# Row table of a fused attention and routed MLP kernel: wide one-hots on two engines, later and more spread out; casts and loads moved

## The chip, the cores and the metric

One core of a Trainium2 chip runs the whole program. The metric is the device time of one execution in microseconds (us), lower is better. The engines are PE (TensorE, matmul), DVE (VectorE), ACT (ScalarE), POOL (GpSimd) and SP (SyncE, which only issues DMAs here). Each engine runs its own instructions strictly in program order and waits on semaphores for the others.

## The reference

```python
B, H, S, D = 8, 8, 576, 64              # batch, heads, sequence, head size
scores = q @ k.T / sqrt(D)              # per batch and head
mask = (row // 64) >= (col // 64)       # block causal, blocks of 64
attn = softmax(where(mask, scores, -1e9))
x = (attn @ v) -> rows of tokens, N = 4608 rows of 512
expert = token_ids * 2654435761 % 8     # 8 experts
out[rows of e] = relu(x[rows of e] @ w1[e]) @ w2[e]   # 512 -> 1024 -> 512
```

Inputs are float32 (token ids int64), the output is float32 [4608, 512].

## The kernel before

The program has two stages. Attention writes its result as bf16 rows to `x_dram`; the expert stage then gathers the rows of each expert in groups of 128 by an index table, `perm3` (128 x 72 integers: one column for each group of 128 slots), multiplies by the two weight matrices and scatters the rows to the output.

**Attention** runs over 32 pairs of heads, `g = 4 b + pr` (batch `b`, pair `pr` of that batch); the loop has 34 steps, because the second half of a pair's work is done two steps later. All engines follow the order in which the code is written (a manual schedule), so a step is a row of instructions in each engine's queue:

- PE: `S_chunk(g, 0..2)` (scores, in PSUM tile `ps`), between them `PV(g-2, 0..1)` (probabilities times V, into the single PSUM tile `O`), at `pr == 0` `S_rest(b)` (the last 64 rows of all four pairs), then `T_pair(g+2)` (transposes q and k of the pair after next into PSUM tile `tp`).
- ACT: one exponential for each chunk (L286), and the two of `S_rest` (L301), once in each batch.
- DVE: `norm(g-2)` (L343 a reciprocal, L346 two multiplications, into tile `xs`), the copy of `tp` into `qkT` (L231), parts of the token routing, casts of q and k of the next batch from float32 to bf16 (L169, L174, tiles `qb` and `kb`), half of the cast of V (L181).
- POOL: the other half of the cast of V (L182, L183, into `vx`; L189 once in each batch), and the DMAs that write a finished batch of `xs` to `x_dram` (`write_x`, L356 and L358, four steps' work in one go at `pr == 1` of the next batch).
- SP: the loads of q, k and v. One batch is 3.54 MB of float32. Each of the tiles `qf`, `kf`, `vf` has two buffers, so that a load of batch b + 2 waits until the casts of batch b have read theirs. A load of `kf` is two DMAs of 512 KB (L109) and two of 64 KB (L116, the last 64 rows).

**Routing** turns the token ids into slots. `route()` is a generator, cut by `yield` into pieces: experts of all tokens, a running count (L399), base offsets through two small matmuls (L407, L408), and the slot number of each token, split into column `shi` (slot // 128) and row `slo` (slot % 128). Then `place(b)`, one call for each batch b, builds `perm3`: for each of five groups of up to 128 tokens it makes a one-hot of the row (`ohp`, 128 x 128, L497) and two of the column times the token number's high and low part (`ohg`, 128 x 72, L499 twice), and a matmul of the two adds each token number to its place; L505 adds the sum of the batch to `acc`. That is 16 DVE instructions and 5 matmuls in one step. `placed()` turns `acc` into `perm3`.

In the order of the steps, `route()` has its first piece ahead of the loop and the others in steps 0 to 3, `place(0)` to `place(7)` are in steps 4 to 11, and `placed()` is in step 12. The loads of q and k of batch 1 are issued ahead of the loop, and the first casts of batch 1 (L169, L174) are in step 0. Ten buffers `xg` for the gathered rows are set to zero on POOL at the very start (L535).

```python
        if g + 2 < NPAIRS:
            T_pair(g + 2)
        if g < 4:
            next(rgen, None)
        elif g < 4 + B:
            place(g - 4)
        elif g == 4 + B:
            placed()
```

Of the kernel before, what the change touches and what calls it, by code (L numbers as in the profile page):

```python
# [7 lines left out]
ALU = mybir.AluOpType  # L8
# [26 lines left out]
def kernel(  # L35
# [334 lines left out]
    def route():  # L370
# [7 lines left out]
        pr = psO.tile([P, 2, 512], F32, name="O", tag="O")[:, 0, 0:325].rearrange("p (i d) -> p i d", i=5)  # L378
        for i in range(5):
            n = P if i < NT else 64  # L380
            nc.tensor.matmul(pr[0:n, i, 0:B], lhsT=eb[:, 128 * i : 128 * i + n],
                             rhs=identbf[0:B, 0:B], start=True, stop=True)
# [4 lines left out]
        nc.vector.tensor_copy(et[0:64, NT, :], pr[0:64, NT, 0:B])
        T = 5 * B
        etf = et[:].rearrange("p i b -> p (i b)")
# [55 lines left out]
        nc.vector.tensor_copy(shi[:], sj[:])  # L445
        nc.vector.tensor_single_scalar(sj[:], si[:], 127, op=ALU.bitwise_and)
        nc.vector.tensor_copy(slo[:], sj[:])

        tokf = rt.tile([P, 5, B], F32, name="tokf")
        nc.gpsimd.iota(tokf[:], pattern=[[P, 5], [S, B]], base=1, channel_multiplier=0,  # L450
                       allow_small_or_imprecise_dtypes=True)
        pidx = rt.tile([P, 1], F32, name="pidx")
        cidx = rt.tile([P, 1], F32, name="cidx")
        nc.gpsimd.iota(pidx[:], pattern=[[0, 1]], base=0, channel_multiplier=1,
                       allow_small_or_imprecise_dtypes=True)
        for c in range(4):
            nc.gpsimd.memset(cidx[32 * c : 32 * c + 32, :], float(c))

        inner = rt.tile([P, 1], F32, name="inner")
        nc.vector.tensor_single_scalar(cidx[:], cidx[:], -127.0, op=ALU.mult)  # L460
        nc.vector.scalar_tensor_tensor(out=inner[:], in0=pidx[:], scalar=4.0, in1=cidx[:],
                                       op0=ALU.mult, op1=ALU.add)
        tok = rt.tile([P, 5, B], I32, name="tok")
        tj = rt.tile([P, 5, B], I32, name="tj")
        nc.vector.tensor_scalar(tok[:, 0:NT, :], tokf[:, 0:NT, :], inner[:, 0:1], None, op0=ALU.add)
        nc.vector.tensor_scalar(tok[:, NT, :], tokf[:, NT, :], pidx[:, 0:1], None, op0=ALU.add)
# [14 lines left out]
        nc.vector.tensor_single_scalar(tj[:], tok[:], 6, op=ALU.arith_shift_right)  # L481
        nc.vector.tensor_copy(vhi[:], tj[:])
        nc.vector.tensor_single_scalar(tj[:], tok[:], 63, op=ALU.bitwise_and)
        nc.vector.tensor_copy(vlo[:], tj[:])
# [52 lines left out]
    load_qk(0, 0, 2, rest=False, engs=(nc.sync, nc.scalar))  # L537
    load_qk(0, main=False, engs=(nc.sync, nc.scalar))
    load_qk(0, 2, 8, rest=False, engs=(nc.sync, nc.scalar))
    load_v(0)  # L540
# [225 lines left out]
```

## Time and profile before

| | |
|---|---|
| median of 3 runs | 375.94 us (374.07 to 376.49) |
| the profiled execution | 375.76 us |
| its span, first to last instruction | 374.1 us |
| busy: PE / DVE / ACT / POOL | 290.7 / 187.8 / 147.0 / 165.7 us |
| exponentials, first start | 19.02 us |
| exponentials, last end | 185.86 us |
| first gather of the expert stage, start | 201.97 us |
| bytes moved by DMA | 64.60 MB |

The profiled execution took 375.76 us, 1.66 us more than its span; the rest lies around the first and last instruction. The expert stage starts when the last rows of attention are in `x_dram`, so the table splits the span into attention (up to about 200 us) and the expert stage (about 174 us). In attention, the exponentials of L301 mark the batches: they stand at the end of step 4b.

### The profile page before, as it was taken

How to read it: one execution, taken by the hardware profiler on the slowest of the kernel's cores; microseconds unless marked ns; L12 is line 12 of the kernel's file. 1: busy time of each engine (PE TensorE's matmuls, PEld its weight loads, DVE VectorE, ACT ScalarE, POOL GpSimd, SP SyncE). 2: the span in 40 equal slices, each digit the busy share in tenths (PEclk: the TensorE clock that was granted, in tenths of full speed). 3: DMA queues.
4: the chain of work that ended last, by engine and by line, in shares of the span. 5: the costliest groups of instructions: out<-in, count | busy, mean ns of one | idle time of the engine just before them, and what ended most of it. 6: DMA issues, size and time to landing. Idle time of an engine off the chain costs nothing. (4 is left out here: it accounts for less than half of the span.)

```text
span 374.1 us, 8170 instructions
## 1 busy us (share of the span) xinstructions
PE 290.7 (78%) x3311; PEld 210.1 (56%) x3311; DVE 187.8 (50%) x496; ACT 147.0 (39%) x177; POOL 165.7 (44%) x249
## 2 busy tenths in 40 slices
PE   0356677777668996989920799999999999999992
PEld 0234454455446774766720489495958586767640
DVE  7767977666776995869430220404141313232141
ACT  1054433344434996788910055050414132322300
POOL 6136106200800754739424724737465655614252
PEclk9999556567666999899995599999999999999997
DMA  8999695059226898968722399869696969744532
GB/s 193 300 260 257 151 288 133 11 154 225 66 91 163 196 256 194 277 166 169 157 52 75 90 179 224 206 178 203 190 206 187 194 213 196 222 98 141 129 135 83
DMA packets 67047, 64.60 MB, mean 173 GB/s; under 512 B 19378, under 2 KB 60340, under 8 KB 64960
## 3 DMA queue, kind: packets, MB, share of 16 engines
q0 software_dynamic: 12288, 35.71, 40.0%
q1 hardware_dynamic: 52064, 27.17, 29.1%
q10 hardware_dynamic: 2656, 1.18, 1.3%
q8 instruction: 26, 0.43, 0.5%
q14 instruction: 13, 0.11, 0.1%
HBM read 67.15 MB, written 15.20 MB: 220 GB/s over the span
## 5 line engine op out<-in xcount | busy, mean ns | idle before, releaser
L286 ACT ACTIVATE pt<-ps 128x1024 bf16<-128x1024 f32 x96 | 95.6, 1023 | 81.8 <-PE ps L262 79.4
L649 ACT ACTIVATE hT<-hp 128x640 bf16<-128x640 f32 x64 | 45.0, 703 | 116.9 <-PE hp L644 116.9
L644 PE MATMUL hp<-xT,w1b 128*128 128x320 bf16 x512 | 73.5, 305 | 0.6 <-DVE xT L633 0.6
L644 PEld LDWEIGHTS <-w1b 128*128 128x128 bf16 x512 | 70.1, 145 | 3.8 <-issue 1.1
L659 PE MATMUL yp<-w2b,hT 128*128 128x512 bf16 x320 | 70.2, 379 | 0.0
L356 POOL DMA_DIRECT2D x_dram<-xs x32 | 24.5, 772 | 79.1 <-DVE xs L346 78.5
L633 DVE COPY xT<-tpx 128x512 bf16<-128x512 bf16 x40 | 15.7, 422 | 79.8 <-PE tpx L632 77.8
L666 POOL DMA_INDIRECT out_dram<-ysb,perm x40 | 39.7, 992 | 35.6 <-DVE ysb L664 26.8
L664 DVE COPY ysb<-yp 128x512 f32<-128x512 f32 x40 | 27.6, 691 | 51.7 <-PE yp L659 50.7
L326 PE MATMUL O<-vx,pt 128*128 128x65 bf16 x896 | 47.0, 212 | 7.5 <-DVE xs L346 5.4
L659 PEld LDWEIGHTS <-hT 128*128 128x128 bf16 x320 | 31.1, 98 | 36.1
L620 POOL DMA_INDIRECT xg<-x_dram,perm x40 | 40.6, 1015 | 16.7 <-issue 11.9
L326 PEld LDWEIGHTS <-pt 128*128 128x128 bf16 x896 | 38.4, 109 | 12.3 <-DVE xs L346 3.8
L238 PE MATMUL ps<-qkT 64*128 64x64 bf16 (+2 forms) x384 | 41.4, 301 | 3.2 <-ACT pt L286 2.4
L182 POOL CAST vx<-vf 64x256 bf16<-64x256 f32 x32 | 16.0, 499 | 37.0 <-DMA vf<-in_v_dram 35.6
L262 PE MATMUL ps<-maskq,maskk 64*128 64x64 bf16 (+2 forms) x320 | 30.8, 233 | 1.1 <-issue 1.1
L632 PE MATMUL tpx<-identbf,xg 128*128 128x128 bf16 x160 | 15.2, 229 | 19.3 <-DMA xg<-x_dram,perm 16.1
L346 DVE TENSOR_TENSOR xs<-O,rs 128x320 bf16<-128x320 f32 x64 | 28.4, 485 | 1.1
L231 DVE COPY qkT<-tp 128x1024 bf16<-128x1024 bf16 x32 | 22.1, 689 | 13.7 <-PE tp L226 13.7
L502 PE MATMUL pq<-ohg,ohp 128*128 128x144 bf16 (+1 forms) x40 | 10.4, 260 | 21.3 <-DVE ohg L499 21.3
L632 PEld LDWEIGHTS <-xg 128*128 128x128 bf16 x160 | 10.9, 101 | 23.3 <-DMA xg<-x_dram,perm 17.6
L226 PE MATMUL tp<-identbf,qb 128*128 128x128 bf16 x128 | 15.1, 253 | 10.8 <-DVE qb L169 10.8
(115 smaller groups left out, 294.0 us busy)
## 6 DMA issues: line engine op xcount, KB each, us to landing
vf<-in_v_dram SPq DMA_DIRECT2D x16, 512.0 KB, 7.3
w1b<-in_moe_w_dram POOLq DMA_DIRECT2D x8, 1024.0 KB, 8.3
w2b<-in_moe_w_dram POOLq DMA_DIRECT2D x8, 1024.0 KB, 8.0
qf<-in_q_dram SPq DMA_DIRECT2D x7, 1024.0 KB, 6.7
kf<-in_k_dram SPq DMA_DIRECT2D x14, 512.0 KB, 7.2
x_dram<-xs POOLq DMA_DIRECT2D x32, 128.0 KB, 5.0
qf<-in_q_dram SPq DMA_DIRECT2D x16, 64.0 KB, 5.8
vf<-in_v_dram SPq DMA_DIRECT2D x16, 64.0 KB, 5.8
```

The costliest lines, as they stand in the source:

```text
L238: nc.tensor.matmul(ps[:, m, o0 : o0 + n], lhsT=qk[rows, pr, 1, 128 * kt : 128 * kt + 128], rhs=qk[rows, pr, 0, q0 : q0 + n], start=first, ...
L262: nc.tensor.matmul(ps[prt, m, o0 : o0 + 128 * n].rearrange("p (t h j) -> p t h j", h=2, j=16)[:, :, 0, :], lhsT=maskk[rows, 64:128] if c e ...
L286: nc.scalar.activation(ptv[:, :, 512 * ch : 512 * ch + 512], ps[:], ACT.Exp, scale=SCALE)
L326: nc.tensor.matmul(O[:, t, :], lhsT=pt[:, m * PTW + o0 : m * PTW + o0 + 128], rhs=vx[:, h, i, :], start=(n == 0), stop=(n == t),)
L346: nc.vector.tensor_tensor(out=xs[:, :, 0:DM].rearrange("p t (d h k) -> p h t d k", d=4, h=H)[:, h], in0=O[:, m, :, 0:D].rearrange("p t (k ...
L620: nc.gpsimd.indirect_dma_start(out=xgs[g % (2 * G)][:], out_offset=None, in_=x_dram[:, :], in_offset=bass.IndirectOffsetOnAxis(ap=perm3[:, ...
L632: nc.tensor.transpose(out=tp[:, db, :], in_=xg[:, db * P : (db + 1) * P], identity=identbf[:])
L644: nc.tensor.matmul(hp[:, t, 0:HC], lhsT=w1b[:, db, ft::NFT], rhs=xT[:, db, t * HC : (t + 1) * HC], start=(db == 0), stop=(db == NKT - 1),)
L649: nc.scalar.activation(hT[:, ft, :].rearrange("p (t n) -> p t n", t=2), hp[:, :, 0:HC], ACT.Relu)
L659: nc.tensor.matmul(yp[:], lhsT=hT[:, ft, tt * P : (tt + 1) * P], rhs=w2b[:, ft, :], start=(ft == 0), stop=(ft == NFT - 1),)
L664: nc.vector.tensor_copy(ysb[:], yp[:])
L666: ins = nc.gpsimd.indirect_dma_start(out=out[:, :], out_offset=bass.IndirectOffsetOnAxis(ap=perm3[:, gg : gg + 1], axis=0), in_=ysb[:], in ...
```

## The change

The loads: `load_qk(0)` and `load_v(0)` come ahead of the token ids on SP. `load_v(1)` moves from ahead of the loop to step 0, and the loads of later batches from the end of a batch to its beginning, q and k of batch b + 2 ahead of V of batch b + 1. The zeroing of the ten `xg` moves from the start into steps 6 to 15, one in each.

The casts of batch 0: the pairs 1, 2 and 3 are cast one by one (pair 1 ahead of the loop, pairs 2 and 3 in steps 0 and 1) instead of all at once, and `T_pair(1)` moves behind `S_chunk(0, 2)`. The cast of V of pair g - 1 is done in step g, right ahead of its use, instead of a batch ahead.

The routing: its pieces go to steps 2 to 6 and 8, with small tiles in PSUM slots of `tp` instead of `O`. `place` is split. `place_a(j)` in steps 10, 12, ..., 24 makes all five row one-hots in one DVE instruction (128 x 640) and all five column one-hots in another (128 x 360), and two POOL multiplications (128 x 360 each) form the products with the token number's parts; `place_b(j)`, one step later, has the five matmuls and the addition. The constant tables move to `rows()` in step 7, and `placed()` to step 26.

```diff
-    shi = rt.tile([P, 5 * B], F32, name="shi")
-    slo = rt.tile([P, 5 * B], F32, name="slo")
+    shi = rt.tile([P, B, 5], BF16, name="shi")
+    slo = rt.tile([P, B, 5], BF16, name="slo")
...
-        pr = psO.tile([P, 2, 512], F32, name="O", tag="O")[:, 0, 0:325].rearrange("p (i d) -> p i d", i=5)
+        pr = psT.tile([P, 5, 65], F32, name="pr", tag="tp")
...
-        pb = psO.tile([P, 2, 512], F32, name="O", tag="O")[:, 0, 0:325].rearrange("p (i d) -> p i d", i=5)
+        pb = psT.tile([P, 5, 65], F32, name="pb", tag="tp")
...
-    def place(b):
+    places = {}
+
+    def place_a(b):
         ohp = rt.tile([P, 5, P], BF16, name="ohp", tag="ohp", bufs=2)
+        ohs = rt.tile([P, 5, NG], BF16, name="ohs", tag="ohs", bufs=2)
         ohg = rt.tile([P, 5, 2, NG], BF16, name="ohg", tag="ohg", bufs=2)
+        nc.vector.tensor_tensor(
+            out=ohp[:], in0=iota_p[:, None, :].to_broadcast([P, 5, P]),
+            in1=slo[:, b, :, None].to_broadcast([P, 5, P]), op=ALU.is_equal)
+        nc.vector.tensor_tensor(
+            out=ohs[:], in0=iota_p[:, None, 0:NG].to_broadcast([P, 5, NG]),
+            in1=shi[:, b, :, None].to_broadcast([P, 5, NG]), op=ALU.is_equal)
+        nc.gpsimd.tensor_tensor(
+            out=ohg[:, :, 0, :], in0=ohs[:],
+            in1=vhi[:, b, :, None].to_broadcast([P, 5, NG]), op=ALU.mult)
+        nc.gpsimd.tensor_tensor(
+            out=ohg[:, :, 1, :], in0=ohs[:],
+            in1=vlo[:, :, None].to_broadcast([P, 5, NG]), op=ALU.mult)
+        places[b] = (ohp, ohg)
+
+    def place_b(b):
+        ohp, ohg = places.pop(b)
         pq = psT.tile([P, 512], F32, name="pq", tag="tp")
...
-            nc.vector.tensor_scalar(ohp[0:n, i, :], iota_p[0:n, :], slo[0:n, col], None, op0=ALU.is_equal)
-            for w, val in enumerate((vhi, vlo)):
-                nc.vector.tensor_scalar(
-                    ohg[0:n, i, w, :], iota_p[0:n, 0:NG], shi[0:n, col], val[0:n, i, b : b + 1],
-                    op0=ALU.is_equal, op1=ALU.mult)
...
-    for xg in xgs:
-        nc.gpsimd.memset(xg[:], 0.0)
+    both = (nc.sync, nc.scalar)
+    load_qk(0, 0, 2, rest=False, engs=both)
+    load_qk(0, main=False, engs=both)
+    load_qk(0, 2, 8, rest=False, engs=both)
+    load_v(0)
     nc.sync.dma_start(tid[:], moe_token_ids.rearrange("(b s) -> b s", b=B))
...
-    next(rgen)
-    cast_qk(0, 0, 1, 4, rest=False)
-    cast_qk(0, 1, 1, 4, rest=False)
-    T_pair(1)
-    for pr in range(NP):
-        cast_v(0, pr)
-    cast_v4(0)
-    load_v(1)
+    for w in range(2):
+        cast_qk(0, w, 1, 2, rest=False)
+
+    steps = {g: (lambda: next(rgen, None)) for g in range(2, 9)}
+    steps[7] = rows
+    for j in range(B):
+        steps[10 + 2 * j] = lambda j=j: place_a(j)
+        steps[11 + 2 * j] = lambda j=j: place_b(j)
+    steps[26] = placed
...
+        if g == 0:
+            T_pair(1)
+        if g < 2:
+            for w in range(2):
+                cast_qk(0, w, g + 2, g + 3, rest=False)
         if g + 2 < NPAIRS:
             T_pair(g + 2)
-        if g < 4:
-            next(rgen, None)
-        elif g < 4 + B:
-            place(g - 4)
-        elif g == 4 + B:
-            placed()
+        if g >= 1 and g - 1 < NPAIRS:
+            bv, pv = divmod(g - 1, NP)
+            cast_v(bv, pv)
+            if pv == 0:
+                cast_v4(bv)
+        if g in steps:
+            steps[g]()
...
-        if nxt:
-            cast_v(b + 1, pr)
-            if pr == 3:
-                cast_v4(b + 1)
-                if b + 2 < B:
-                    load_qk(b + 2)
-                    load_v(b + 2)
+        if pr == (1 if b == 0 else 0) and b + 2 < B:
+            load_qk(b + 2)
+        if pr == 0 and b + 1 < B:
+            load_v(b + 1)
+        if 6 <= g < 6 + 2 * G:
+            nc.gpsimd.memset(xgs[g - 6][:], 0.0)
```

The queue of DVE around the first steps, before: `qf_158` is q of batch 0, `qf_175` q of batch 1, `tp_297` the transposes of pair 2.

```order
L373 TENSOR_SCALAR ei_208<-tid_140 8x576
L375 CAST eb_210<-ei_208 8x4x32x4
L377 CAST eb_210<-ei_208 8x64
L169 CAST qb_184<-qf_158 128x3x2x4x64
L169 CAST kb_186<-kf_159 128x3x2x4x64
L231 COPY qkT_188<-tp_221 128x2x512
L181 CAST vx0_115<-vf_170 128x2x4x64 x4
L231 COPY qkT_188<-tp_297 128x2x512
```

The same place after the change: `qf_147` is q of batch 0, `qf_165` and `kf_166` are q and k of batch 1.

```order
L169 CAST qb_174<-qf_147 128x2x4x64
L169 CAST kb_176<-kf_148 128x2x4x64
L231 COPY qkT_178<-tp_259 128x2x512
L169 CAST qb_269<-qf_165 128x2x2x4x64
L174 CAST qb_269<-qf_165 128x256
L169 CAST qb_174<-qf_147 128x2x4x64
L169 CAST kb_176<-kf_148 128x2x4x64
L231 COPY qkT_178<-tp_315 128x2x512
L181 CAST vx0_115<-vf_159 128x2x4x64
L169 CAST kb_330<-kf_166 128x2x2x4x64
L174 CAST kb_330<-kf_166 128x256
L343 RECIPROCAL rs_389<-O_350 128x10
```

The routing left this place, and the casts of batch 1 now stand ahead of the last casts of batch 0 (q) and ahead of the first normalization (k).

The queue of DVE in a step with `place`, before (step 4; the rows of L497 and L499 come four times more).

```order
L231 COPY qkT_478<-tp_723 128x2x512
L497 TENSOR_SCALAR ohp_733<-iota_p_145,slo_142 128x128
L499 TENSOR_SCALAR ohg_734<-iota_p_145,shi_141,vhi_143 128x72
L499 TENSOR_SCALAR ohg_734<-iota_p_145,shi_141,vlo_144 128x72
...
L505 TENSOR_TENSOR acc_146<-acc_146,pq_735 128x144
L169 CAST qb_757<-qf_627 128x2x2x4x64
```

After the change, the queue of DVE in steps 10 and 11.

```order
L231 COPY qkT_1268<-tp_1269 128x2x512
L181 CAST vx0_115<-vf_658 128x2x4x64
L490 TENSOR_TENSOR ohp_1282<-iota_p_145,slo_142 128x640
L493 TENSOR_TENSOR ohs_1283<-iota_p_145,shi_141 128x360
L207 COPY qkT_1268<-tp_1289 128x2x2x64 x2
L169 CAST qb_1084<-qf_649 128x2x2x4x64
L343 RECIPROCAL rs_1345<-O_1306 128x10
L346 TENSOR_TENSOR xs2_139<-O_1306,rs_1345 128x20x16 x2
L231 COPY qkT_1268<-tp_1369 128x2x512
L181 CAST vx0_115<-vf_658 128x2x4x64
L512 TENSOR_TENSOR acc_146<-acc_146,pq_1382 128x144
```

Sixteen instructions of one step became two in an even step and one in the next.

After the change, the queue of POOL in steps 9 to 11 (`xs1` is the finished batch 1; L612 zeroes an `xg`).

```order
L189 CAST v40_116<-vf_658 64x4x64 x2
L356 DMA x_dram_63<-xs1_138 4x32x512 x4
L358 DMA x_dram_63<-xs1_138 64x512
L612 MEMSET xg3_76 128x512
L182 CAST vx0_115<-vf_658 64x2x2x64
L183 CAST vx0_115<-vf_658 64x2x2x64
L496 TENSOR_TENSOR ohg_1284<-ohs_1283,vhi_143 128x5x72
L499 TENSOR_TENSOR ohg_1284<-ohs_1283,vlo_144 128x5x72
L612 MEMSET xg4_77 128x512
```

The V casts of a pair now stand behind the writes of the batch before, and the products of `place_a` behind them.

## Rows read from the trace of the kernel before

**Rows 1.** The page: granted clock of PE in 40 slices of the span, in tenths.

```profile
PEclk9999556567666999899995599999999999999997
```

**Rows 2.** Timeline of ACT: start, length, instruction, count, idle time before it.

```profile
19.02 1.94 ACT L286 ACTIVATE pt<-ps 128x1024 bf16<-128x1024 f32 x2 [12.91 <-PE ps L262]
...
50.66 0.76 ACT L301 ACTIVATE pt<-ps 64x256 bf16<-64x256 f32 x2
...
119.95 0.76 ACT L301 ACTIVATE pt<-ps 64x256 bf16<-64x256 f32 x2
...
133.14 0.76 ACT L301 ACTIVATE pt<-ps 64x256 bf16<-64x256 f32 x2
...
165.11 0.76 ACT L301 ACTIVATE pt<-ps 64x256 bf16<-64x256 f32 x2
...
179.08 0.76 ACT L301 ACTIVATE pt<-ps 64x256 bf16<-64x256 f32 x2
180.03 5.83 ACT L286 ACTIVATE pt<-ps 128x1024 bf16<-128x1024 f32 x6 [0.20 <-ACT pt L301]
```

**Rows 3.** Windows: stretch, length, busy of each engine, PE clock, DMA share, GB/s.

```profile
6.00:42.00 36.00, 18.66 (x244) 12.70 (x245) 27.36 (x80) 11.78 (x14) 11.82 (x33) 0.94 1.15 271
98.33:107.75 9.42, 6.86 (x81) 4.41 (x80) 6.93 (x26) 3.07 (x3) 3.81 (x8) 0.50 0.12 35
121.00:133.10 12.10, 11.69 (x267) 8.99 (x264) 11.58 (x30) 11.34 (x12) 8.58 (x15) 1.00 0.90 217
146.70:165.10 18.40, 14.14 (x285) 10.62 (x285) 12.63 (x29) 12.58 (x15) 9.49 (x15) 0.91 0.95 244
```

**Rows 4.** Groups of instructions by line: busy, mean ns of one, idle before.

```profile
L499 DVE TENSOR_SCALAR ohg<-iota_p,shi,vhi 128x72 bf16<-128x72 bf16 (+1 forms) x40 | 12.1, 303 | 0.0
L497 DVE TENSOR_SCALAR ohp<-iota_p,slo 128x128 bf16<-128x128 bf16 (+1 forms) x40 | 10.0, 251 | 0.0
L505 DVE TENSOR_TENSOR acc<-acc,pq 128x144 f32<-128x144 f32 x8 | 2.4, 304 | 3.0 <-PE pq L502 3.0
L394 DVE TENSOR_TENSOR oh<-et,iota_e 128x320 f32<-128x320 f32 x1 | 0.5, 492 | 0.1
L356 POOL DMA_DIRECT2D x_dram<-xs x32 | 24.5, 772 | 79.1 <-DVE xs L346 78.5
L182 POOL CAST vx<-vf 64x256 bf16<-64x256 f32 x32 | 16.0, 499 | 37.0 <-DMA vf<-in_v_dram 35.6
```

**Rows 5.** Timeline of the start on POOL, DVE and SP.

```profile
1.28 6.09 DVE L70 TENSOR_SCALAR identbf<-jmp 128x128 bf16<-128x128 f32 x1 [1.28 <-POOL jmp L68]
...
2.55 4.74 POOL L535 MEMSET xg<- 128x512 bf16 x10
...
18.85 2.73 SPq L116 DMA_DIRECT2D kf<-in_k_dram  x2
```

**Rows 6.** DMA issues: count, KB each, median us from issue to landing.

```profile
kf<-in_k_dram SPq DMA_DIRECT2D x14, 64.0 KB, 6.2
```

**Rows 7.** Windows, as rows 3: four pieces of the routing, then a step's PE work.

```profile
24.10:25.25 1.15, 0.00 (x0) 0.00 (x0) 1.09 (x5) 0.00 (x0) 0.00 (x0) 1.00 1.23 255
30.97:36.16 5.19, 3.87 (x58) 2.83 (x58) 4.84 (x16) 2.05 (x2) 4.54 (x17) 1.00 1.20 273
39.07:42.74 3.67, 3.67 (x58) 2.81 (x55) 3.32 (x17) 1.67 (x3) 0.00 (x0) 0.50 0.92 224
97.48:102.56 5.08, 5.08 (x69) 3.71 (x68) 2.94 (x7) 2.90 (x3) 4.54 (x10) 0.50 0.30 86
```

**Rows 8.** Timeline of DVE, three normalizations; and of PE, a pause.

```profile
37.43 0.21 DVE L343 RECIPROCAL rs<-O 128x10 f32<-128x10 f32 x1
...
122.51 0.21 DVE L343 RECIPROCAL rs<-O 128x10 f32<-128x10 f32 x1
...
125.44 0.21 DVE L343 RECIPROCAL rs<-O 128x10 f32<-128x10 f32 x1
...
149.51 0.22 PE L226 MATMUL tp<-identbf,kb 128*128 128x128 bf16 x1 [2.99 <-issue]
```

More of the change, by code (lines that the diff above doesn't have):

```diff
@@ L396, in route @@
             in1=iota_e[:, :, None].to_broadcast([P, E, T]), op=ALU.is_equal)
+        yield
         cum = rt.tile([P, E, T], F32, name="cum")
@@ L444, in route @@
         nc.vector.tensor_single_scalar(sj[:], si[:], 7, op=ALU.arith_shift_right)
-        nc.vector.tensor_copy(shi[:], sj[:])
+        nc.vector.tensor_copy(shi[:].rearrange("p b i -> p (b i)"), sj[:])
         nc.vector.tensor_single_scalar(sj[:], si[:], 127, op=ALU.bitwise_and)
[L447 to L466, printed above, removed]
+        nc.vector.tensor_copy(slo[:].rearrange("p b i -> p (b i)"), sj[:])
+        yield
         jo = rt.tile([1, OVT], F32, name="jo")
@@ L479, in route, with rows @@
         nc.vector.tensor_copy(ov_i[:], eof[:])
[L481 to L484, printed above, removed]
+    def rows():
+        nc.gpsimd.iota(vhi[:], pattern=[[9, B], [2, 5]], base=0, channel_multiplier=0,
+                       allow_small_or_imprecise_dtypes=True)
+        pidx = rt.tile([P, 1], F32, name="pidx")
+        cidx = rt.tile([P, 1], F32, name="cidx")
+        nc.gpsimd.iota(pidx[:], pattern=[[0, 1]], base=0, channel_multiplier=1,
+                       allow_small_or_imprecise_dtypes=True)
+        for c in range(4):
+            nc.gpsimd.memset(cidx[32 * c : 32 * c + 32, :], float(1 - 127 * c))
         nc.gpsimd.iota(iota_p[:], pattern=[[1, P]], base=0, channel_multiplier=0,
@@ L533 @@
     NPAIRS = B * NP
-    for xg in xgs:
-        nc.gpsimd.memset(xg[:], 0.0)
+    both = (nc.sync, nc.scalar)
[3 more added lines that the diff above has]
+    load_v(0)
     nc.sync.dma_start(tid[:], moe_token_ids.rearrange("(b s) -> b s", b=B))
[L537 to L540, printed above, removed]
     load_qk(1)
     rgen = route()
-    cast_qk(0, 0, 0, 1, rest=False)
-    cast_qk(0, 1, 0, 1, rest=False)
+    for w in range(2):
+        cast_qk(0, w, 0, 1, rest=False)
     T_pair(0)
-    cast_qk(0, 0, 0, 0)
-    cast_qk(0, 1, 0, 0)
+    for w in range(2):
+        cast_qk(0, w, 0, 0)
     T_rest(0)
-    next(rgen)
-    cast_qk(0, 0, 1, 4, rest=False)
-    cast_qk(0, 1, 1, 4, rest=False)
-    T_pair(1)
-    for pr in range(NP):
-        cast_v(0, pr)
-    cast_v4(0)
-    load_v(1)
+    for w in range(2):
+        cast_qk(0, w, 1, 2, rest=False)
[5 more added lines that the diff above has]
+    steps[26] = placed
     for g in range(NPAIRS + 2):
@@ L573 @@
                 S_rest(b)
+        if g == 0:
+            T_pair(1)
+        if g < 2:
+            for w in range(2):
+                cast_qk(0, w, g + 2, g + 3, rest=False)
         if g + 2 < NPAIRS:
             T_pair(g + 2)
-        if g < 4:
-            next(rgen, None)
-        elif g < 4 + B:
-            place(g - 4)
-        elif g == 4 + B:
-            placed()
+        if g >= 1 and g - 1 < NPAIRS:
[5 more added lines that the diff above has]
+            steps[g]()
         if nxt:
```

21 lines of the change are left out of this document (12 added, 9 removed).

## The prediction

> **What bounds the kernel now.** I read the page's clock line first. The expert stage runs at 2.4 GHz nearly throughout and nothing in it is changed, so its 174 us stay. Attention is where the clock sits at half [rows 1]. Next the timeline of ACT, as a milestone for each batch: the exponentials of `S_rest` stand at 50.66 us for batch 1, 119.95 for batch 3, 133.14 for batch 4, 165.11 for batch 6, 179.08 for batch 7, and the last exponential ends at 185.86 [rows 2]. Batches 1 and 2, which hold the eight `place` steps, take 69.29 us, batch 3 takes 13.19. So 43 us of the span hang on `place` and the clock that goes with it.
>
> The windows say why. From 98.33 to 107.75, a step with `place`, no engine is full: PE 6.86 of 9.42, DVE 6.93, ACT 3.07, clock 0.50, DMA nearly idle [rows 3]. The work goes round in a ring: PE transposes, DVE copies, makes fifteen small one-hots, and PE stands behind each of them in order. In batch 3 (121.00 to 133.10) PE, DVE and ACT are all at 94 to 97% and the clock is 2.4 GHz [rows 3]: 13.2 us is about what ACT allows, and DVE has next to no room.
>
> The start is the second place: DVE's first instruction takes 6.09 us, until 7.37, while POOL zeroes the `xg` back to back until 7.29 [rows 5]. The third is the loads: from 6 to 42 us DMA moves 271 GB/s without a break [rows 3]; more it does not show over such a stretch.
>
> **The change, part by part.** I follow the milestones; everything after attention moves along one to one.
>
> *Start, to batch 1's milestone.* Without the zeroing DVE is free some 4.7 us earlier, and `S_chunk(0)` no longer stands behind `T_pair(1)` and the first routing piece, so the first exponential (19.02 us [rows 2]) comes earlier too, by up to some 9 us, an estimate (4.7, and as much for the routing and the wide casts that stood ahead of it). Not all of this is kept. The casts of batch 1 stand ahead of the last casts of batch 0 and of the first normalization, and DVE waits there for the loads. The last pieces of `kf` of batch 1 are issued until 18.85 + 2.73 = 21.58 and land some 6.2 us later [rows 5, 6], at 27.8, or about 27.3 with the token ids no longer ahead. The first normalization then comes at about 28 instead of 37.43 [rows 8]. From there to batch 1's milestone I add up as much as before: the second half of the routing is gone from it, its first pieces and the PE round trip of the token ids have come in. So the milestone moves from 50.66 to about 41, a gain of **9.5 us**. Bounds: 5 (kf later by a load's delay) and 14 (the whole 9 us, and the routing hidden).
>
> *Batches 1 and 2, steps 5 to 12.* A step without routing takes PE 5.1 us at 1.2 GHz: from the first score matmul of step 9 to its last transpose, 97.48 to 102.56, busy throughout [rows 7]; at 2.4 GHz 3.3 (13.19 / 4); DVE alone needs 2.93 (122.51 to 125.44 between two normalizations [rows 8]). Step 5 carries the long routing piece, 30.97 to 36.16 = 5.2 us [rows 7]; with 2.93 that is 8, since DVE is one queue and the next normalization stands behind it. Step 4 has the count, 1.15 us [rows 7], for which PE waits in order, behind the copy and the V cast that DVE has before it: 2.2 more than 5.1, 7.3. Steps 6 and 8 share the last stretch of routing, 3.67 us of which some 3.0 stay [rows 7]: 5.2 and 4.5 us. Steps 7 and 9 carry almost nothing: 4.2, between the two clocks; steps 11 and 12 are as below. The milestone stands behind the scores of its step, so the eight stretches from batch 1's to batch 3's are 7.3 + 8.0 + 5.2 + 4.2 + 4.5 + 4.2 + 2 x 3.83 = **41.1 us** instead of 69.29. Bounds: 35 (clock up at once, no step over its DVE work) and 51 (5.1 or more in every step).
>
> *`place` itself.* Fifteen instructions of 251 to 303 ns and an addition of 304 become two, one step ahead of the matmuls [rows 4]. For a two-tensor operation of DVE the rows give 492 ns for 320 columns and 304 for 144 [rows 4], so about 1.07 ns a column and 150 fixed: 0.83 us for 640 columns, 0.54 for 360. No row shows this form with bf16 alone; it could be half of that, hardly more. With the addition 1.67 us for two steps, some 1.45 in starts. On PE it is five matmuls whose inputs were made a step earlier, no longer a ring.
>
> DVE had no room in batch 3, so this is not free: 12.0 us a batch plus 2 x 1.45 = 14.9. The loads ask for more: 3.54 MB of q, k, V and 0.59 MB of `x_dram` rows are 4.13 MB, at 271 GB/s 15.3 us. The re-timed loads start with the batch and have five steps to land, so they can follow one another without a pause, but a batch cannot be shorter: **15.3 us**, 3.83 a step. Before, batches 4 to 6 (as milestones, 119.95 to 165.11) took 45.16; three of mine take 45.9, a loss of **0.7**. Bounds: 13.3 each, the rate of the undisturbed batch, and 18.4, the one from 146.70 to 165.10 with DMA 0.95 busy [rows 3], in which PE also stood 2.99 us with nothing that the trace shows to wait for [rows 8].
>
> *POOL.* The products are new. POOL's nearest row is a cast, 499 ns for 256 columns [rows 4], so 0.7 us for 360 columns with one input; for two I take 0.9 to 1.4 us each. Per batch POOL then has casts 4.9, writes 3.7 (five DMAs at up to 772 ns), two `place_a` 4 to 5: 13 to 14 of 15.3. That hides, but not by much: the V cast of the pair at `pr == 1` stands behind the writes and has about 1 us to spare before `PV` wants it. POOL and DVE get in each other's way (the 6.09 us above is the extreme), which I count inside the bounds of the batch. As to this the Trainium skill, "GPSIMD Engine Reference" (When to use GPSIMD, and Key points), says that GpSimd shares its SBUF interfaces with VectorE, in contention with VectorE's two-port and two-input instructions, and is about half as fast in two-input elementwise work; the zeroing that held up DVE agrees, the two-input rate no run here shows. By the figure in its section "Elementwise — side-by-side cycle accounting", 4497 ns for 2048 elements with two inputs, a product would be some 0.8 us (an estimate); if DVE stood still for all sixteen the sum would be 13 us longer.
>
> The zeroing, ten of about 0.47 us, goes to steps 6 to 15, where POOL has room in most; at worst it costs DVE 2 or 3 us there, inside the bounds.
>
> *End.* Steps 24 and 25 still hold `place`: 14.8 instead of 13.97 from 165.11 to 179.08. The V casts of batch 7 now run in the last steps, 0.7 more in the last 6.78 us. The tail (last normalization, writes, gathers) is unchanged.
>
> **The sum.** 9.5 + (69.29 - 41.1) - 0.7 - 0.8 - 0.7 = 35.5 us. The profiled execution took 375.76 us, beside a median of 375.94, so 375.76 - 35.5 = **340.3 us**, last exponential at 150 instead of 185.86.
>
> **Rivals.**
>
> *The loads don't bind, the clock comes up early.* The ring is gone from step 4 on, and PE at 94% holds 2.4 GHz in batch 3. With batches at 14 us (DVE and ACT) and steps 5 to 12 at 35: 340.3 - 6 - 5 = 329. Against it: 271 GB/s is all that the loads reach over 36 us.
>
> *The loads bind harder.* Every batch behaves like 146.70 to 165.10: 18.4 us for each of batches 3 to 6, and pauses of PE that drop its clock. 340.3 + 3 x 3.1 + 3.5 = 353. For it: DMA is now near full throughout; against it: batch 3, with DMA at 0.90, took 13.2 [rows 2, 3].
>
> *The low clock was the cost, not `place`.* If PE stays at 1.2 GHz, a batch is 4 x 5.1 and 0.8 for the two rest pieces, 21.2, whoever waits for whom. Six batches from 41 us on, and 8 us of routing, put batch 7 at 176 instead of 179.08, and its slower end takes this back: 375, no change. Against it: PE at 1.2 GHz would then be busy without a break, and in batch 3, where it is, the clock is up [rows 3].
>
> *POOL holds DVE.* This is the one that ends slower. DVE's first two instructions stood still as long as POOL's queue had no gap [rows 5]. Two products behind each other are such a stretch, and the casts of q and k come right behind `ohs`. To eat the 35.5 us, eight `place_a` must each cost 4.4 us more, 2.2 a product beyond the 0.9 to 1.4: from 3.3 us a product on (9 ns a column, where a cast takes 2) the change loses. At 4 us: 340.3 + 8 x 2 x 2.9 = 387.
>
> **How the numbers follow.** Forecast 0.64, loads that don't bind 0.14, loads that bind harder 0.14, low clock 0.04, POOL 0.04. A measurement of this kernel tells about 1% from no change: the three runs spread over 0.6%. Faster by over 1%: 0.92; within: 0.04, the low clock; slower: 0.04. The range reaches to the two neighbours of the forecast, 326 to 355: the start's bounds give +-4.5, the eight steps +-7, the later batches -6 to +9, which together are about +-12.
>
> **What the profile after would show.** Right: L70 under 1 us; first exponential near 10 us; then a pause of DVE for `qf` and `kf` at about 18 to 28; `S_rest` of batch 1 near 41, of batch 3 near 82, of batch 6 near 128; PE clock at 1.00 from about step 8; L490 and L493 near 0.8 and 0.5 us; POOL products about 1 us each and over before PE reaches `place_b`. Wrong: a clock of 0.5 in steps 10 to 25; PE waiting for `ohg`; casts of L169 stretched far over 0.7 us beside products; batches of 18 us with DMA at 0.95; PE waiting in `PV` for `vx`, which POOL casts late behind the writes.

## The result and the profile after

The changed kernel takes **362.23 us** (median of 4 runs, 360.49 to 363.59) beside 376.22 us for the kernel before (374.07 to 377.47): ratio 0.963, 95% interval 0.957 to 0.970. It is faster by 14 us where 35.5 were forecast; the forecast of 340.3 us and its range (326 to 355) both miss. The profiled execution took 360.49 us, its span 358.9.

The clock line of the page after, 40 slices; [rows 1] has the same line of before.

```profile
PEclk9997886989899899969855999999999999999997
```

The clock is no longer at half for a third of attention, but it still dips in single slices up to the end of attention. The timeline of ACT gives the milestones of the batches, as in [rows 2] (start, length, instruction, count, idle time before it).

```profile
9.71 1.94 ACT L286 ACTIVATE pt<-ps 128x1024 bf16<-128x1024 f32 x2 [2.93 <-PE ps L262]
...
41.08 0.76 ACT L301 ACTIVATE pt<-ps 64x256 bf16<-64x256 f32 x2
...
83.41 0.75 ACT L301 ACTIVATE pt<-ps 64x256 bf16<-64x256 f32 x2
...
103.90 0.75 ACT L301 ACTIVATE pt<-ps 64x256 bf16<-64x256 f32 x2
...
141.05 0.76 ACT L301 ACTIVATE pt<-ps 64x256 bf16<-64x256 f32 x2
...
161.34 0.76 ACT L301 ACTIVATE pt<-ps 64x256 bf16<-64x256 f32 x2
...
170.89 2.18 ACT L286 ACTIVATE pt<-ps 128x1024 bf16<-128x1024 f32 x2 [0.77 <-PE ps L262]
```

First exponential near 10 us, batch 1 at 41.08 (forecast 41), batch 3 at 83.41 (forecast 82.1): up to here the forecast holds. Batch 6 was to come near 128 and comes at 141.05; batch 7 at 161.34 instead of 143. So 17 of the missing 20 us are lost in batches 3 to 6. The windows of these four, columns as in [rows 3], and of two short stretches of batch 3:

```profile
83.41:103.90 20.49, 15.19 (x294) 11.69 (x294) 15.26 (x35) 12.91 (x15) 13.61 (x23) 0.92 0.79 204
103.90:122.98 19.08, 15.20 (x294) 11.79 (x294) 15.42 (x35) 12.90 (x15) 12.13 (x19) 0.91 0.87 219
122.98:141.05 18.07, 13.87 (x294) 10.76 (x294) 15.40 (x35) 12.92 (x15) 12.35 (x19) 1.00 0.65 154
141.05:161.34 20.29, 15.85 (x289) 11.93 (x289) 14.91 (x35) 12.92 (x15) 13.14 (x23) 0.83 0.88 191
...
92.00:96.00 4.00, 0.71 (x14) 0.59 (x14) 3.36 (x8) 1.41 (x2) 3.76 (x7) 0.96 0.58 127
96.00:100.00 4.00, 4.00 (x66) 3.02 (x65) 1.43 (x4) 1.82 (x2) 3.70 (x8) 0.62 0.86 276
```

18 to 20.5 us a batch instead of 15.3, and no engine is full on average: DVE is busy for 14.9 to 15.4 us, POOL for 12.1 to 13.6, DMA has a share of 0.65 to 0.88, not 0.95. That is the picture of a wait, not of a bound. It stands at 92 to 96 us: PE works 0.71 of 4 us while POOL is busy for 3.76. In the next 4 us PE is busy throughout, at a clock of 0.62: what follows the pause runs partly at 1.2 GHz. The pauses are the larger part of the loss: the batch from 122.98 us takes 18.07 us at a clock of 1.00. The waits from 60 to 172 us (engine, line, waited for: us, times, longest) name the releaser.

```profile
POOL ohg L496 <- DVE ohs L493: 23.7, 5, 6.4
...
PE O L326 <- POOL vx L183: 13.7, 8, 3.3
PE O L326 <- DVE vx L181: 5.6, 14, 0.7
```

The group of the `PV` matmuls in the two traces, before and after (busy, mean ns of one, idle before), shows that the wait for POOL's cast was 1.2 us and is 13.7 us now:

```profile
L326 PE MATMUL O<-vx,pt 128*128 128x65 bf16 x896 | 47.0, 212 | 7.5 <-DVE xs L346 5.4 <-POOL vx L183 1.2 <-issue 0.9
L326 PE MATMUL O<-vx,pt 128*128 128x65 bf16 x896 | 47.2, 205 | 23.9 <-POOL vx L183 13.7 <-DVE vx L181 7.5 <-DVE xs L346 2.3
```

And the timeline of batch 3 shows how the wait is made: of the rows from 84 to 97 us, most of POOL's queue (what is left out of it are two zeroings, two halves of V casts and, at its end, the next two products), and the PE row that waits.

```profile
85.66 1.10 POOL L496 TENSOR_TENSOR ohg<-ohs,vhi 128x360 bf16<-128x360 bf16 x1 [5.18 <-DVE ohs L493]
...
86.73 0.83 POOL L499 TENSOR_TENSOR ohg<-ohs,vlo 128x360 bf16<-128x360 bf16 x1
...
87.97 0.39 POOL L182 CAST vx<-vf 64x256 bf16<-64x256 f32 x1
...
88.87 1.30 POOL L189 CAST v<-vf 64x256 bf16<-64x256 f32 x2
...
90.12 2.79 POOL L356 DMA_DIRECT2D x_dram<-xs  x4
...
92.90 0.56 POOL L358 DMA_DIRECT2D x_dram<-xs  x1
...
94.67 0.95 POOL L183 CAST vx<-vf 64x256 bf16<-64x256 f32 x1
...
95.67 0.93 PE L326 MATMUL O<-vx,pt 128*128 128x65 bf16 x14 [3.29 <-POOL vx L183]
```

POOL first sits idle for 5.18 us, because the products stand at the head of its queue and DVE has not made `ohs` yet. From 85.66 on it works without a gap: two products, a V cast, the cast of `v4`, five writes, another V cast, and the next two products behind that. The last V cast, which ends 10 us into this pile, is the one that PE needs: PE stood before `PV` for 3.29 us.

The new operations themselves, by groups (busy, mean ns of one, idle before), beside [rows 4, 5]:

```profile
L496 POOL TENSOR_TENSOR ohg<-ohs,vhi 128x360 bf16<-128x360 bf16 x8 | 8.5, 1060 | 23.9 <-DVE ohs L493 23.7
L499 POOL TENSOR_TENSOR ohg<-ohs,vlo 128x360 bf16<-128x360 bf16 x8 | 6.9, 860 | 0.0
L490 DVE TENSOR_TENSOR ohp<-iota_p,slo 128x640 bf16<-128x640 bf16 x8 | 6.7, 844 | 0.0
L493 DVE TENSOR_TENSOR ohs<-iota_p,shi 128x360 bf16<-128x360 bf16 x8 | 4.8, 600 | 0.0
...
L512 DVE TENSOR_TENSOR acc<-acc,pq 128x144 f32<-128x144 f32 x8 | 2.3, 294 | 0.0
L70 DVE TENSOR_SCALAR identbf<-jmp 128x128 bf16<-128x128 f32 x1 | 1.4, 1430 | 1.3 <-POOL jmp L68 1.3
```

On average 844 and 600 ns where 0.83 and 0.54 us were worked out, 0.86 and 1.06 us for a product where 0.9 to 1.4 were allowed, and the start's 6.09 us [rows 5] gone down to 1.43 (under 1 was the sign named). The prices of the new operations were about right; the place in the queue was not.

### The profile page after: what moved, and what is told of

The parts are those of the page before. It is cut to its first block, busy times and chain, and to the rows that moved or that the text cites. A ratio compares the mean times of both kernels' runs of the same rounds, so it can differ in the third digit from the quotient of the medians.

```text
span 358.9 us, 8081 instructions
## 1 busy us (share of the span) xinstructions
PE 281.0 (78%) x3311; PEld 205.7 (57%) x3311; DVE 169.5 (47%) x390; ACT 148.9 (41%) x177; POOL 178.8 (50%) x265
## 5 line engine op out<-in xcount | busy, mean ns | idle before, releaser
L286 ACT ACTIVATE pt<-ps 128x1024 bf16<-128x1024 f32 x96 | 97.5, 1023 | 63.6 <-PE ps L262 60.2
L656 PE MATMUL hp<-xT,w1b 128*128 128x320 bf16 x512 | 72.3, 302 | 0.7 <-DMA w1b<-in_moe_w_dram 0.5
L326 PE MATMUL O<-vx,pt 128*128 128x65 bf16 x896 | 47.2, 205 | 23.9 <-POOL vx L183 13.7
L678 POOL DMA_INDIRECT out_dram<-ysb,perm x40 | 39.7, 992 | 35.7 <-DVE ysb L676 26.9
L645 DVE COPY xT<-tpx 128x512 bf16<-128x512 bf16 x40 | 15.7, 421 | 79.7 <-PE tpx L644 77.7
L356 POOL DMA_DIRECT2D x_dram<-xs x32 | 23.3, 733 | 40.5 <-DVE xs L346 40.0
L238 PE MATMUL ps<-qkT 64*128 64x64 bf16 (+2 forms) x384 | 39.5, 289 | 3.5 <-ACT pt L286 3.1
L182 POOL CAST vx<-vf 64x256 bf16<-64x256 f32 x32 | 15.1, 473 | 23.3 <-DMA vf<-in_v_dram 22.4
L496 POOL TENSOR_TENSOR ohg<-ohs,vhi 128x360 bf16<-128x360 bf16 x8 | 8.5, 1060 | 23.9 <-DVE ohs L493 23.7
```

Of the source, the lines that this page charges most:

```text
L238: nc.tensor.matmul(ps[:, m, o0 : o0 + n], lhsT=qk[rows, pr, 1, 128 * kt : 128 * kt + 128], rhs=qk[rows, pr, 0, q0 : q0 + n], start=first, ...
L286: nc.scalar.activation(ptv[:, :, 512 * ch : 512 * ch + 512], ps[:], ACT.Exp, scale=SCALE)
L326: nc.tensor.matmul(O[:, t, :], lhsT=pt[:, m * PTW + o0 : m * PTW + o0 + 128], rhs=vx[:, h, i, :], start=(n == 0), stop=(n == t),)
L656: nc.tensor.matmul(hp[:, t, 0:HC], lhsT=w1b[:, db, ft::NFT], rhs=xT[:, db, t * HC : (t + 1) * HC], start=(db == 0), stop=(db == NKT - 1),)
L678: ins = nc.gpsimd.indirect_dma_start(out=out[:, :], out_offset=bass.IndirectOffsetOnAxis(ap=perm3[:, gg : gg + 1], axis=0), in_=ysb[:], in ...
```

## The experiments

Theory A: the loss is the pile on POOL (the work that stands in its queue) ahead of the V cast, which the change puts only one step ahead of its use. The rivals are told in each expectation.

**V cast one step earlier.** The only edit to the changed kernel:

```diff
-        if g >= 1 and g - 1 < NPAIRS:
-            bv, pv = divmod(g - 1, NP)
-            cast_v(bv, pv)
-            if pv == 0:
-                cast_v4(bv)
+        if g < NPAIRS:
+            cast_v(b, pr)
+            if pr == 0:
+                cast_v4(b)
```

> The changed kernel with V of pair g cast in step g instead of g + 1, so two steps ahead of its use; nothing else is changed. Theory A (POOL's queue: in the third step of each batch PV waits for a V cast that stands behind the writes to x_dram and the products of place_a, and the pause then costs PE its clock as well): the pauses before PV, 13.7 us for POOL's half of the cast and 7.5 us for DVE's half in the changed kernel, nearly vanish, a batch takes about 15.5 us instead of 19.5, and the time falls from 362 to about 342 us (337 to 347). Theory B (DVE is full, and it and POOL hold each other up, so that the batch takes 19 to 20 us anyhow): the pauses move to another place, 357 to 362 us. Theory C (the loads set the batch): no change, 360 to 364 us.

Measured: 344.83 us, ratio 0.919 (0.914 to 0.923). One step of lead gives back some 17 us, and theory A has its total. The edit moves DVE's half of the cast as well as POOL's, so the 17 us are not POOL's alone; the writes on SP's queue, below, leave DVE's half where it was. Of the waits from 60 to 160 us, that of `PV` for L183 is gone, and another has become the longest of PE:

```profile
PE pq L509 <- POOL ohg L499: 10.7, 8, 2.0
DVE rs L343 <- PE O L331: 9.9, 8, 1.6
...
PE O L326 <- DVE xs L346: 3.1, 4, 1.5
```

PE now stands ahead of the placing matmuls for POOL's products, 1.3 us each time. Batches 4 and 5 still take 17.71 and 17.57 us at a clock of 0.90, where theory A had 15.5:

```profile
97.98:115.69 17.71, 14.60 (x294) 11.41 (x294) 16.07 (x35) 12.63 (x15) 12.24 (x19) 0.90 0.94 235
115.69:133.26 17.57, 14.66 (x294) 11.43 (x294) 15.88 (x35) 12.64 (x16) 12.25 (x19) 0.90 0.81 196
```

**The row table's change alone.** New routing steps, `place_a` and `place_b`; the start, the loads, the zeroing and the V casts (a batch ahead) as in the kernel before.

```diff
+    for xg in xgs:
+        nc.gpsimd.memset(xg[:], 0.0)
...
+        if nxt:
+            cast_v(b + 1, pr)
+            if pr == 3:
+                cast_v4(b + 1)
+                if b + 2 < B:
+                    load_qk(b + 2)
+                    load_v(b + 2)
```

> The new routing steps and the split place_a and place_b of the changed kernel alone; the casts of batch 0, the casts of V a batch ahead, the order of all loads and the zeroing of xg at the start are those of the kernel before. Theory A: V is cast early enough that POOL's queue holds nobody up, so most of the gain that was forecast comes without the re-timed casts: about 353 us (346 to 360), faster than the whole change. Theory B: the batches with place_a take 19 to 20 us as in the changed kernel and the start is as slow as before, 365 to 371 us. Theory C: the loads are issued late as before, 360 to 368 us.

Measured: 350.68 us, ratio 0.935 (0.931 to 0.939), in theory A's range. Less of the change is 12 us faster than all of it, so the re-timed casts, loads and zeroing together lose time as they stand. What they gain at the start is seen in the milestones: batch 1 at 44.53 us here, 41.08 in the changed kernel. But the batches are no shorter than with the V cast moved, and here DVE is nearly full, with the same 35 instructions; batch 3:

```profile
83.35:102.26 18.91, 15.20 (x296) 11.61 (x295) 17.57 (x35) 12.82 (x15) 12.39 (x19) 0.89 0.97 248
```

The longer time of DVE lies mostly in its casts: over batches 3 and 4 its half of a V cast (L181) takes 763 ns on average, in the changed kernel 469.

**The writes on SP's queue**, to take 3.4 us out of the pile.

```diff
-            nc.gpsimd.dma_start(
+            nc.sync.dma_start(
...
-        nc.gpsimd.dma_start(x_dram[S * b + 512 : S * b + S, :], xs[0:64, NT, :])
+        nc.sync.dma_start(x_dram[S * b + 512 : S * b + S, :], xs[0:64, NT, :])
```

> The changed kernel with the five writes of a batch to x_dram issued from SP's queue instead of POOL's; V is still cast one step ahead of its use. Theory A: without 3.6 us of writes ahead of it POOL's half of the V cast comes in time in the third step, the long pauses (2 to 3.3 us) go, the short waits for DVE's half stay: about 346 us (340 to 352). Theory B: 357 to 362 us. Theory C: the writes now stand in the queue of the loads and hold some of them up, 362 to 368 us.

Measured: 359.51 us, ratio 0.960 (0.955 to 0.964): the total misses theory A's range and lies in B's. The windows of two batches (POOL is the last of the five engines) show what A expected of the pauses:

```profile
99.23:116.74 17.51, 14.17 (x294) 10.82 (x294) 15.83 (x35) 12.94 (x16) 8.26 (x14) 1.00 0.90 235
116.74:134.25 17.51, 14.17 (x294) 10.82 (x294) 15.82 (x35) 12.93 (x16) 8.26 (x14) 1.00 0.83 217
```

PE's wait for L183 falls from 13.7 to 2.1 us, with no pause over 0.8, the low clock is gone, and the milestone of batch 7 comes at 151.28 instead of 161.34. So the five writes in POOL's queue cost the changed kernel some 10 us. 7.6 of them are lost again behind the program's last scatter: it is issued at 342.24 us and the span ends 13.7 us later, in the changed kernel at 352.83 and 6.1 us later, and from 348 us on the trace shows nothing at work. Without that loss the total would be some 352 us, the upper end of theory A's range: a batch still takes 17.5 us.

**The products on DVE**, to take 1.9 us out of the pile and to end POOL's wait for `ohs`.

```diff
-        nc.gpsimd.tensor_tensor(
+        nc.vector.tensor_tensor(
             out=ohg[:, :, 0, :], in0=ohs[:],
...
-        nc.gpsimd.tensor_tensor(
+        nc.vector.tensor_tensor(
             out=ohg[:, :, 1, :], in0=ohs[:],
```

> The changed kernel with the two products of place_a on DVE instead of POOL: POOL loses about 1.9 us in every second step and no longer waits for DVE's one-hots there, DVE gains about 1.0 us. Theory A: POOL runs ahead of the casts again, its writes start some 2 us earlier, the pause shrinks to under 1 us: about 351 us (345 to 357), although DVE has more to do. Theory B: DVE is the bound and now has 2 us more in each batch, 364 to 372 us. Theory C: 360 to 364 us.

Measured: 362.22 us, ratio 0.960 (0.953 to 0.966): no gain; theories A and B miss, and the total is that of theory C, no change. PE's wait for L183 falls from 13.7 to 4.8 us, as A has it, but the waits for DVE's own half of the V cast (L181) grow from 5.6 to 9.3 us:

```profile
85.16:104.19 19.03, 13.79 (x294) 10.72 (x294) 17.20 (x39) 12.93 (x16) 11.05 (x18) 1.00 0.79 204
```

In this window of batch 3 DVE has 17.2 of 19.0 us; the next two batches take 19.46 and 20.82 us at clocks of 0.87 and 0.75. What POOL gives up, DVE cannot take here: both halves of the V cast stand one step ahead of `PV`, each behind its engine's own pile.

Four more start from the kernel with the V cast one step earlier, to find what holds a batch at 17.6 us. **Without the row table** (its one-hots, products, matmuls and sums are left out; theory D lays the rest on their work, E on something else, F on PE's pauses before the placing matmuls).

```diff
     for j in range(B):
-        steps[10 + 2 * j] = lambda j=j: place_a(j)
-        steps[11 + 2 * j] = lambda j=j: place_b(j)
+        pass
```

> The kernel of v_cast_one_step_earlier without the one-hot operations, products, matmuls and adds of the row table (so no token is gathered or written back; its expert stage and its total are not to be read, only the batches up to the last exponential). Theory D, the row table's work on VectorE and GpSimd is what makes a batch 17.6 us instead of 15.3: batches 4 to 6 take 15.0 to 15.8 us each. Theory E, the 17.6 us come from elsewhere (loads, the exponentials, the order of the transposes): they stay at 16.8 or more. Theory F, only the pause of TensorE in front of the placing matmuls costs: 16.2 to 16.8 (17.6 less the pause of 1.3 us).

Measured, in one run: 12.95 us for batch 3, then 16.98, 17.09 and 17.72. For batches 4 to 6 this is theory E's number, 16.8 or more, and the loads are among its causes; the 12.95 of batch 3 no theory has. Two of the windows:

```profile
77.10:90.05 12.95, 12.62 (x284) 9.79 (x284) 12.42 (x29) 12.37 (x16) 10.61 (x17) 1.00 0.97 241
...
107.03:124.12 17.09, 13.91 (x284) 10.66 (x284) 12.18 (x29) 12.40 (x15) 9.01 (x15) 0.90 1.02 253
```

And the wait of DVE from 90 to 142 us:

```profile
DVE vx L181 <- DMA vf<-in_v_dram: 8.3, 3, 3.0
```

As long as loads are in hand a batch takes 13 us and DVE 12.2 to 12.4; then DVE waits three times for V itself, DMA is full (1.02), and the clock falls to 0.90. So the loads do bind a kernel that asks for a batch in 13 us; whether they still do at 16 us is the question of the last runs.

**The placing matmuls one step later** (two steps behind the one-hots), with everything kept.

```diff
-        steps[10 + 2 * j] = lambda j=j: place_a(j)
-        steps[11 + 2 * j] = lambda j=j: place_b(j)
-    steps[26] = placed
+        steps[10 + 2 * j] = lambda j=j: (place_b(j - 1) if j else None, place_a(j))
+    steps[26] = lambda: (place_b(B - 1), placed())
```

> v_cast_one_step_earlier with the placing matmuls of a group two steps behind its one-hot operations instead of one. Theory F, TensorE's pauses for the products (10.7 us in 8 times) and the clock that falls behind them cost a batch about 1.0 to 1.3 us: 344.8 - 8 = 337 us (333 to 341). Theory D, VectorE's own work sets the batch and TensorE only waits there instead of elsewhere: 344 us (342 to 346), the pauses for GpSimd's products gone, pauses for VectorE's V cast in their place.

Measured: 341.43 us, ratio 0.908 (0.904 to 0.912), 3.4 us less than with the V cast alone, between the two theories. The pauses for the products are gone. The V cast moved and the writes on SP's queue, then both leads (that of the V cast and that of the placing matmuls) and the writes on SP's queue:

> v_cast_one_step_earlier with the writes of x on SP's queue. In writes_on_sp the span ended 12.6 us behind the last scatter's issue instead of 5.1: 7.5 us at the program's end that the profile does not explain; both theories expect them again. Theory F, GpSimd's queue still delays the products: batches of 16.6 to 17.0 and with the longer end 344.8 + 7.5 - 6 = 346 us (343 to 349). Theory D, VectorE's work binds: batches stay at 17.4 to 17.7, total 352 us (350 to 354).

> v_cast_one_step_earlier with both edits: the placing matmuls two steps behind, the writes of x on SP. Theory F: batches of 16.3 to 16.7, total 344.8 + 7.5 - 9 = 343 us (340 to 346). Theory D: batches of 17.3 to 17.6, total 352 us (349 to 354).

Measured: 349.50 us (ratio 0.930, 0.926 to 0.934), between the two theories, and 349.65 us (0.931, 0.926 to 0.936), in theory D's range. Batches 3 to 6 take 16.0 to 17.5 us in both, which is neither theory's number throughout. The last exponential ends at 153.7 and 153.1 us. With the V cast alone it ended at 157.8, so there the writes on SP's queue bring 4 us, and the longer end takes 7.5; with both leads it ended at 153.7 already, and they bring next to nothing. The span ends 13.6 us behind the last scatter's issue both times.

Last, V or DVE? **V queued ahead of q and k** on SP, and **no V load after batch 1** (the casts take batch 1's V again, so that the output is that of another V).

```diff
+        if pr == 0 and b + 1 < B:
+            load_v(b + 1)
         if pr == (1 if b == 0 else 0) and b + 2 < B:
             load_qk(b + 2)
-        if pr == 0 and b + 1 < B:
-            load_v(b + 1)
```

```diff
     def load_v(b):
+        if b >= 2:
+            loaded[b][2] = loaded[1][2]
+            return
```

> v_cast_early_place_b_later (341.4 us) with the next batch's V load queued on SP ahead of the q and k of the batch after that, which are wanted later. Theory G, what is left of a batch's excess (16.6 us instead of 15.3) is lateness of V on the load queue: the stalls in batches 5 and 6 and the low clock behind them go, 338 us (335 to 340). Theory H, the queue's total or VectorE's work binds: 341 us (340 to 343), whatever the order.

> v_cast_early_place_b_later without the loads of V from batch 2 on, the casts taking batch 1's V again, so that the queue carries 2.36 MB a batch for q and k instead of 3.54 MB with V; everything else is done. If the loads set the batch: batches 3 to 6 at 15.0 to 15.6 us. If VectorE's work sets it: they stay at 16.3 to 16.8 us.

On that chip the kernel before took 392.49 us, so the totals (361.19 us, ratio 0.916, 0.909 to 0.924; and 359.79) are not to be set beside the others; the batches are. The windows of batches 3 to 6 without the V loads:

```profile
78.78:94.80 16.02, 13.51 (x296) 10.43 (x294) 15.46 (x35) 12.50 (x15) 14.20 (x24) 1.00 0.75 184
94.80:111.24 16.44, 13.70 (x296) 10.51 (x294) 16.06 (x35) 12.40 (x16) 13.38 (x22) 1.00 0.73 188
111.24:127.55 16.31, 13.51 (x296) 10.43 (x294) 15.95 (x35) 12.50 (x15) 12.18 (x19) 1.00 0.53 126
127.55:142.94 15.39, 13.32 (x292) 10.27 (x291) 14.84 (x36) 12.40 (x15) 12.33 (x21) 1.00 0.54 110
```

A third of the load is gone, DMA falls to 0.53, and batches 3 to 5 stay at 16.0 to 16.4 us, not at 15.0 to 15.6: DVE, with 15.95 of 16.31, sets them. The two versions that do all the work, side by side on another chip:

> v_cast_early_place_b_later beside v_queued_ahead_of_qk on one chip, because the latter ran in a job in which the kernel before took 392.5 us and not 375 to 376. If the expert stage of that chip alone was longer, the ratio to the kernel before is again 0.905 to 0.915 here.

> Theory G, V's lateness on the load queue still cost: 2 us or more under place_b_later_same_chip. Theory H, VectorE's work binds (as no_v_load_after_batch_1 has it): within 1.5 us of it.

340.43 us (ratio 0.910, 0.904 to 0.917) and 340.58 us (0.908, 0.903 to 0.914) beside 375.31: no difference, as theory H has it. The windows of batches 3 to 5 of the first:

```profile
78.22:94.24 16.02, 13.50 (x296) 10.41 (x294) 15.46 (x35) 12.51 (x15) 14.20 (x24) 1.00 1.02 251
94.24:110.58 16.34, 13.75 (x296) 10.52 (x294) 15.66 (x35) 12.51 (x16) 11.90 (x20) 1.00 1.01 250
110.58:126.88 16.30, 13.52 (x296) 10.44 (x294) 15.63 (x35) 12.52 (x16) 12.42 (x22) 1.00 0.94 231
```

They are the same 16.02, 16.3 and 16.3 us, with the whole of V loaded. On the chip of the first run (341.43 us) the same kernel had 17.51 and 17.43 us for batches 4 and 5:

```profile
93.66:111.17 17.51, 15.10 (x296) 11.44 (x294) 15.79 (x35) 12.51 (x16) 11.32 (x19) 0.90 1.01 259
111.17:128.60 17.43, 14.83 (x296) 11.32 (x294) 15.96 (x35) 12.51 (x16) 13.79 (x23) 0.90 0.83 209
```

There the clock fell behind pauses of PE of up to 1.55 us; whether late loads made them was not tested on that chip. So DVE's work sets the batch where the clock stays at 1.00. The two versions are the best found, 9% under the kernel before and about 6% under the changed one.

## Why the prediction was wrong

Stretch by stretch, in us, from the milestones (forecast; the changed kernel; with the V cast one step earlier; with the placing matmuls later as well, on the chip of the last two runs):

| stretch | forecast | changed | V cast earlier | and place later |
|---|---|---|---|---|
| start to batch 1 | 41 | 41.1 | 39.7 | 40.2 |
| batches 1, 2 | 41.1 | 42.3 | 40.1 | 38.0 |
| batches 3 to 5 | 45.9 | 57.6 | 53.4 | 48.7 |
| batch 6 | 14.8 | 20.3 | 14.9 | 15.4 |
| batch 7 to the last exponential | 10.3 | 11.7 | 9.7 | 9.7 |
| from there to the span's end | 185.4 | 185.8 | 185.9 | 185.6 |

The fifth row's 10.3 is 9.6 + 0.7. The prediction put it as 6.78 + 0.7, with the last exponential at 185.86, as the table of the kernel before has it too, because its row was cut off there [rows 2]; in full the row before reads

```profile
180.03 8.67 ACT L286 ACTIVATE pt<-ps 128x1024 bf16<-128x1024 f32 x9 [0.20 <-ACT pt L301]
```

and ends at 188.70. As the sum was one of differences, only that milestone is touched (150 should have been 153).

*Right: start and batches 1, 2.* 9.5 us were forecast and 9.6 came, by the way that was forecast: DVE waits for the last of batch 1's k until 26.53 us and the first normalization follows at 26.74 (about 28 forecast). The eight steps took 42.3 us for 41.1. The ring of PE and DVE was the cost: with the row table's change alone they take 38.8 us instead of 69.29. The clock is not at 1.00 from step 8 on, as the prediction had it, but at 0.79 and 0.91 in these two batches.

*Wrong: the POOL paragraph, "That hides, but not by much ... about 1 us to spare before `PV` wants it".* It added up POOL's work over a batch, 13 to 14 of 15.3 us, and that was right (12.1 to 13.6). But the work does not stand evenly: the products wait for DVE's `ohs` (5.18 us in batch 3), and then 10 us of work stand in one piece up to the end of a cast that PE wants. PE waits 13.7 us for it from 60 to 172 us, up to 3.29 at a time, with a stretch at a granted clock of about 0.6 behind it. The sign was named among those that would show the forecast wrong, and costed at nothing in the sum. Giving the cast, both halves of it, one more step is worth 17 us (0.963 to 0.919); taking the writes alone out of the pile brings batch 7's milestone 10 us forward.

*Wrong, the same kind: "over before PE reaches `place_b`".* The products come to PE one step after the one-hots, and with the V cast out of the way PE waits for them 1.3 us each time. Two steps of lead are worth 3.4 us more. With both leads the time is 340.4 and 341.4 us, which is the forecast: the size was that of a schedule which the change doesn't have, and it agrees in part by luck, as the next paragraph shows.

*Mis-sized, and why the forecast still came out with both leads: the later batches at 15.3 us, the larger of DVE's 14.9 and the loads' 15.3.* With both leads batches 3 to 5 take 16.0 to 16.3 us on the chip of the last two runs, and DVE is busy for 15.5 to 15.7 of them. They are DVE's: taking the V loads away leaves them as they are. The base of 12.0 was right (12.15 to 12.4 without the row table), and so was the table's own price: from the start of its addition to that of the operation behind its last one-hot DVE needs 1.39 us (95.12 to 96.51) and 1.59 (103.04 to 104.63), and 1.45 were put. What the sum left to its bounds is that DVE's casts get longer with the products on POOL (over two batches L174 on q takes 874 ns on average with the row table and 484 without it, L181 488 and 422), and that DVE stands idle for 0.6 to 0.7 us in each of these batches. Shorter first steps (38.0 instead of 41.1) make up for it. Whether the loads' 15.3 is a floor stays open: without the row table and with DMA full, batches took 17 us, part of it pauses of DVE for V.

*The rivals.* "The loads bind harder", 353, lies nearest the time, but its mechanism isn't the one: DMA has 0.65 to 0.88 in the slow batches, and neither order nor amount of V's load changes a batch with both leads. "POOL holds DVE" has the right engine and, in the changed kernel, the wrong victim: products of 0.86 and 1.06 us on average are far from 3.3, and it was PE that waited. Where V was cast a batch ahead, with the row table's change alone, DVE's own work grew, to 17.57 us in batch 3 where it is 15.46 with both leads; that POOL did this was not tested apart. "The loads don't bind", 329, needs batches of 14 us: without the row table one batch took 12.95 us, with it none of batches 3 to 6 took less than 14.9. "The low clock was the cost" is out: without the ring the clock came up to 0.79 and 0.91 in batches 1 and 2, and the eight steps were 27 us shorter. On the products' price the Trainium skill, "GPSIMD Engine Reference" ("Elementwise — side-by-side cycle accounting"), led to an estimate of 0.8 us; the quickest here, at 95.71 and 96.45 us among others, took 0.78 each, and the longest, at 134.15 us, 1.30, so the page's figure is the lower end.

## What to carry to other kernels

Where two engines feed a third, costs summed over a batch say only whether the work fits, not whether it comes in time: lay out the queue of the helping engine from the point at which it may start, and ask at what moment its last consumer wants each piece. When an operation is moved on an engine that goes in order, give what others wait for a lead longer than the largest pile that can stand before it. Here one step of lead was worth 17 us. A pause of PE is paid twice where the clock falls behind it, as to 0.62 behind the pause at 92 to 96 us. And a total that agrees with a forecast proves no term of it: compare stretch by stretch.

## What the runs showed of the hardware

- With the writes of `x_dram` on SP's queue the span ends 13.6 to 13.7 us behind the issue of the last scatter, in three kernels of three; with the writes on POOL's queue 6.0 to 6.4 us. From some 6 us behind that issue on no engine and no DMA is at work in the trace. Why is open.
- A cast of DVE beside POOL's products took longer: L174 on q took 0.88 us at 86.03, beside the products at 85.66 and 86.73; the group before has 311 ns on average, after 608.
- One kernel, the one with V queued ahead, had a span of 360.2 us on one chip and 338.9 on another, with the last exponential at 152.9 and 151.8: 20 us of the difference lie in the expert stage, whose matmuls by the first weights (L654) took 324 and 302 ns on average and had 12.4 and 1.3 us of idle time before them.
